# Block-causal attention and gated MLP in one kernel: scores of both heads as single-pass products in the two 64-row halves of the array, seven slots and one output run a pair of heads

## The chip, the cores and the metric

The kernel runs on one core of a Trainium2 chip. The time is device time in microseconds (us) of one execution, from the first instruction to the last, as the runs report it; the number to be predicted is the median over runs of the changed kernel.

The core has five instruction streams that work side by side and meet at semaphores. TensorE (PE in the rows) multiplies: its instructions are a matmul and the load of the weights for it (PEld). VectorE (DVE), ScalarE (ACT) and GpSimd (POOL) work elementwise, and SyncE (SP) only issues DMA transfers here. A tile of numbers lies on 128 partitions; an operand of a matmul is contracted over its partitions, which are the rows of TensorE's array, and the weights' columns are the columns of the array. The results come into eight PSUM banks of 128 x 512 float32.

## The reference

Eight batches, eight heads, 576 tokens, 64 channels a head. The attention is causal in blocks of 64 tokens; its output is the input of a gated MLP that mixes tokens.

```python
B, H, S, D = 8, 8, 576, 64
scores = q @ k.T / sqrt(D)
scores = where(pos_q // 64 >= pos_k // 64, scores, -1e9)
scores = scores - max(scores, axis=-1)
attn = exp(scores)
attn = attn / (sum(attn, axis=-1) + 1e-9)
x = concatenate_heads(attn @ v)                 # [8, 576, 512]

h = maximum(x @ w_in, 0)                        # w_in [512, 1024]
u, v = h[..., :512], h[..., 512:]
v_n = (v - mean(v)) / sqrt(var(v) + 1e-6)       # over the 512 channels
v_s = w_spatial @ v_n + b_spatial               # over the 576 tokens, w_spatial [576, 576]
out = (u * v_s) @ w_out                         # w_out [512, 512]
```

## The kernel before, in words

**Two streams in one program.** The attention goes pair of heads by pair of heads: 8 batches of 4 pairs, written (batch, pair). When a batch has its four pairs, its MLP is cut into 29 groups of products (`moe`: 5 v groups at L468, 8 u groups at L537, 8 spatial groups `ms` at L560, 8 output groups `mo` at L581), and these are put between the attention steps of the next batch's pairs. The MLP of the last batch stands alone at the end.

**Two precisions.** TensorE multiplies whole float32 in several passes and rounded numbers (float32r) in one. Most products are made from two rounded parts of each operand, hi and lo (lo = value - hi), as hi x hi + hi x lo + lo x hi.

**Operands of the scores.** For a pair, q and k of both heads are transposed on the host into one array of 128 rows (64 channels of the one head above 64 channels of the other) by 1216 columns: k in 0 to 576, q in 576 to 1088, and in 1088 to 1216 query block 8 (the last 64 tokens) of both heads, with zeros in the other head's rows. `load_pair` fetches it into `raw`. In batch 0 the scores are made from `raw`, whole, one instruction a tile over the 64 rows of its head (L293). From batch 1 on `prep_pair` makes hi on ScalarE (L222) and lo on VectorE (one of four pieces, two in the first pair) and POOL (L225), and ten DMAs on SyncE (L235 to L243) stack them, for each head, into a tile `st` of 128 rows: k's hi part twice, q's hi above q's lo, and k's lo part twice. Two products over all 128 rows, L296 and L297, then give all combinations of parts for one tile of one head.

**Nine steps a pair.** `TILES` lists the score tiles: (head, query tile), where tile t has 128 queries and needs 128 (t + 1) keys; head 2 stands for query block 8 of both heads. One step is: the scores of a tile into a bank of `ps_s`; a subtraction from the mask and a minimum over the keys on VectorE (L298, or L319 in two halves for block 8), which leaves the masked scores in `p` and the minimum in `nmax`; the exponential with the sum of a row on ScalarE (L325); a small sum and a reciprocal on VectorE (L331, L334); the division on POOL (L338). Three steps later (five in the first 30 steps) `transposes` puts the tile's 128 x 128 blocks through TensorE into a bank of `ps_t`, and a copy takes them to `ptlo` (VectorE, L369), `pthi` or `ptc4` (ScalarE, L376 to L389).

**Two output runs a pair.** `av_lo` (L415) multiplies v by the transposed weights of query tiles 0 and 1, a step after tile (1, 1)'s transposes; `av_hi` (L430, L434, L439) those of the rest, a step after the pair's last transposes. Each uses 64 columns of the array a head; both write the one bank of `ps_av`. `x_evac` copies the bank on ScalarE (L404, rounded) and subtracts on VectorE (L405, the lo part of x).

**What sets the order.** The step loop at the end of the function issues the instructions: scores of step n, work ahead (the next pair's loads and splits, and in batch 0 the decoding of the MLP's weights from float64, `prep_w`, spread over fixed steps), then transposes and output runs that are due, then as many MLP groups as a credit of 29/36 a step allows. From this each engine gets its own row of instructions; a framework then puts in the semaphores, and an instruction that waits holds up all that is behind it on its engine. Buffers are reused in turn: 3 banks for scores, 2 for transposes, 1 for outputs, 2 for the MLP, 4 tiles of `p`, 1 tile each of hi and lo, 3 of `st`. In batch 0, while no MLP runs, its buffers and banks hold more of `p` and `s` in flight (`p_tile`, `s_bank`).

## Time and profile before

| what | value |
|---|---|
| three runs | 762.03, 762.12 and 763.51 us, median 762.12 |
| span of the profiled execution | 760.0 us |
| TensorE busy, share of the span | 750.3 us, 99% |
| VectorE busy | 486.7 us, 64% |
| ScalarE busy | 453.3 us, 60% |
| POOL busy | 316.7 us, 42% |
| chain of waits, share on TensorE | 87% |
| moved by DMA | 96.37 MB in 43814 packets |

The profile is of one execution. Its span, 760.0 us, goes from the first to the last recorded instruction; the runs' own time has 2.1 us more at the median. In rows of the trace "L296" is line 296 of the kernel; `s<-st` is a result and its operands by the program's names (batch, pair and tile numbers left out); `128*64 128x320` is the part of the array in use and the shape of the moving operand. Matmuls are pipelined: a record begins when the instruction starts and its end is modelled, so records overlap, and the cost of a product to TensorE is read from the differences of starts. A product in float32 may leave one record for each pass.

### The profile page before, as it was taken

How to read it: one execution, taken by the hardware profiler on the slowest of the kernel's cores; microseconds unless marked ns; L12 is line 12 of the kernel's file. 1: busy time of each engine (PE TensorE's matmuls, PEld its weight loads, DVE VectorE, ACT ScalarE, POOL GpSimd, SP SyncE). 2: the span in 40 equal slices, each digit the busy share in tenths (PEclk: the TensorE clock that was granted, in tenths of full speed). 3: DMA queues.
4: the chain of work that ended last, by engine and by line, in shares of the span. 5: the costliest groups of instructions: out<-in, count | busy, mean ns of one | idle time of the engine just before them, and what ended most of it. 6: DMA issues, size and time to landing. Idle time of an engine off the chain costs nothing.

```text
span 760.0 us, 16034 instructions
## 1 busy us (share of the span) xinstructions
PE 750.3 (99%) x5284; PEld 648.9 (85%) x5284; DVE 486.7 (64%) x1744; ACT 453.3 (60%) x1236; POOL 316.7 (42%) x478
## 2 busy tenths in 40 slices
PE   8999899999999999999999999999999999999998
PEld 5567798988888889988888889988889988888898
DVE  6997985668545785448755487555865568543641
ACT  6786766655665656566656566655666556654232
POOL 4785775423444325443344334433344423423011
DMA  6477585555465445464355554456454554430001
GB/s 216 138 212 219 146 232 128 129 134 124 114 171 125 115 119 135 133 173 111 85 141 150 141 124 103 127 152 159 106 130 116 139 146 112 92 77 33 0 9 55
DMA packets 43814, 96.37 MB, mean 127 GB/s; under 512 B 6866, under 2 KB 15570, under 8 KB 43732
## 3 DMA queue, kind: packets, MB, share of 16 engines
q1 hardware_dynamic: 43732, 95.35, 48.4%
q8 instruction: 42, 0.69, 0.4%
q14 instruction: 40, 0.33, 0.1%
HBM read 38.18 MB, written 9.44 MB: 63 GB/s over the span
## 4 chain that ended last, share of the span: by engine, by line
PE 87%; DVE 7%; ACT 2%; issue 2%; DMA 1%; SPq 0%; DVEq 0%; ACTq 0%
PE mo L581 14%; PE ms L560 13%; PE mu L537 12%; PE mv L468 11%; PE avh L430 7%; PE t L375 6%; PE s L297 4%; PE s L296 4%; PE s L315 3%; PE avl L415 3%; PE t L382 2%; PE t L368 2%; PE mv L479 1%; PE avh L434 1%; DVE p L298 1%
## 5 line engine op out<-in xcount | busy, mean ns | idle before, releaser
L338 POOL TENSOR_SCALAR p<-p,ssum 128x384 f32<-128x384 f32 (+4 forms) x288 | 175.0, 615 | 252.0 <-DVE ssum L334 96.6
L325 ACT ACTIVATE p<-p,nmax 128x384 f32<-128x384 f32 (+4 forms) x288 | 168.5, 586 | 59.4 <-DVE nmax L298 38.7
L298 DVE CUSTOM_DVE_ANT_0 p<-s,mask 128x128 f32<-128x128 f32 (+3 forms) x256 | 122.7, 486 | 60.2 <-PE s L297 46.4
L537 PE MATMUL mu<-x,wi_hi 128*128 128x288 f32 x512 | 116.3, 303 | 0.5 <-DVE vr L485 0.5
L537 PEld LDWEIGHTS mu<-x,wi_hi 128*128 128x128 f32 x512 | 85.4, 188 | 2.9 <-ACT pthi L376 1.0
L468 PE MATMUL mv<-wi_hi,x 128*128 128x512 f32 x256 | 85.9, 396 | 0.0
L225 POOL TENSOR_TENSOR lo<-raw,hi 128x288 fp32r<-128x288 f32 (+1 forms) x83 | 68.3, 837 | 37.4 <-ACT hi L222 37.4
L331 DVE TENSOR_SCALAR ssum<-ssum 128x1 f32<-128x1 f32 (+1 forms) x224 | 39.1, 175 | 63.8 <-ACT p L325 63.3
L560 PE MATMUL ms<-ws_hi,vh 128*128 128x288 f32 x256 | 78.6, 307 | 0.0
L560 PE MATMUL ms<-ws_hi,vl 128*128 128x288 f32 x256 | 75.4, 294 | 0.0
L560 PE MATMUL ms<-ws_lo,vh 128*128 128x288 f32 x256 | 75.3, 294 | 0.0
L581 PE MATMUL mo<-gh,wo_hi 128*128 128x288 f32 x256 | 74.5, 314 | 0.5 <-ACT gh L568 0.5
L376 ACT COPY pthi<-t 128x384 f32<-128x384 f32 (+1 forms) x128 | 67.8, 530 | 9.9 <-PE t L375 9.1
L568 ACT CAST gh<-u 128x288 fp32r<-128x288 f32 x64 | 27.7, 433 | 75.1 <-DVE u L567 72.7
L297 PE MATMUL s<-st 128*128 128x128 f32 (+1 forms) x224 | 72.3, 323 | 0.0
L296 PE MATMUL s<-st 128*128 128x128 f32 (+1 forms) x224 | 71.5, 321 | 0.0
L375 PE MATMUL t<-ident,p 128*128 128x128 f32 x448 | 70.8, 275 | 0.4 <-POOL p L338 0.3
L537 PE MATMUL mu<-x,wi_lo 128*128 128x288 f32 x256 | 69.7, 295 | 0.0
L581 PE MATMUL mo<-gh,wo_lo 128*128 128x288 f32 x256 | 69.7, 295 | 0.0
L569 POOL TENSOR_TENSOR gl<-u,gh 128x288 fp32r<-128x288 f32 x48 | 38.7, 806 | 64.6 <-ACT gh L568 63.8
L430 PE MATMUL avh<-pthi,v 128*64 128x320 f32 x384 | 61.0, 441 | 0.4 <-DVE x L405 0.4
L375 PEld LDWEIGHTS t<-ident,p 128*128 128x128 f32 x448 | 52.3, 141 | 8.6 <-issue 3.0
(119 smaller groups left out, 1726.0 us busy)
## 6 DMA issues: line engine op xcount, KB each, us to landing
raw<-qk SPq DMA_DIRECT2D x31, 608.0 KB, 5.0
st<-lo SPq DMA_DIRECT2D x112, 144.0 KB, 3.1
st<-hi SPq DMA_DIRECT2D x56, 272.0 KB, 3.2
v<-v SPq DMA_DIRECT2D x32, 320.0 KB, 3.4
outT<-o SPq DMA_DIRECT2D x64, 144.0 KB, 2.5
st<-hi SPq DMA_DIRECT2D x56, 144.0 KB, 3.1
...
```

The costliest lines, as they stand in the source:

```text
L225: (nc.vector if n < (2 if (b, pr) == (1, 0) else 1) else nc.gpsimd).tensor_tensor(out=lo[:, cs], in0=raw[:, cs], in1=hi[:, cs].bitcast(F32 ...
L296: nc.tensor.matmul(ps[:, :n], st[:, qs], st[:, Q8:Q8 + n], start=True, stop=False)
L297: nc.tensor.matmul(ps[:, :n], st[:, qs], st[:, :n], start=False, stop=True)
L298: nc.vector.tensor_tensor_reduce(out=pt[:, :n], in0=ps[:, :n], in1=mask[:, 512 - n:], scale=-0.125, scalar=BIG, op0=ALU.add, op1=ALU.min, ...
L325: nc.scalar.activation(pt[:, :n], pt[:, :n], AF.Exp, bias=mx, scale=-1.0, accum_out=ssum[:, sc:sc + 1])
L338: nc.gpsimd.tensor_scalar(out=pk[:, :nk], in0=pk[:, :nk], scalar1=ssum[:, 2 + sc - k:3 + sc - k], scalar2=1.0, op0=ALU.mult, op1=ALU.mult,)
L375: nc.tensor.transpose(bk[:, c, :], pt[:, c * P:(c + 1) * P], ident)
L430: nc.tensor.matmul(av[js, 0:320], vt[:, c, js], hi[:, j, c, :], start=(c == 0), stop=False)
L468: nc.tensor.matmul(ps, xs[k][:, j, cs], w[:, k, DH:], start=(n == 0), stop=(n == 3 * NC - 1),)
L537: nc.tensor.matmul(ps[:, :HT], w[:, k, ds], xs[k][:, j, zs], start=(n == 0), stop=(n == 3 * NC - 1),)
L560: nc.tensor.matmul(ps[:, :HT], a[:, ds], w[:, k, zs], start=(n == 0), stop=False)
L581: nc.tensor.matmul(ps[:, :HT], w[:, k, es], a[:, k, :], start=(n == 0), stop=(n == 3 * ND - 1),)
```

## The change

**Seven slots in the place of nine steps.** `SLOTS` lists (head, first tile, last tile): slots 0 and 1 hold query tiles 0 and 1 of a head together (in one bank, 128 and 256 columns, and one tile of `p`), slots 2 and 3 tile 2, slots 4 and 5 tile 3, slot 6 query block 8 of both heads. Slot n of a pair makes the minima and exponentials (`exps`) of slot n, the sums and the division (`norm`) of slot n - 1 and the transposes of slot n - 2.

**Scores in runs, half by half.** `scores` has no stacked operands: a head's products take its 64 rows of hi and lo, three products a tile (hi x hi, hi x lo, lo x hi), and the heads take turns, so that a product in rows 0 to 63 stands beside one in rows 64 to 127. Slots 0 to 3 are issued together at slot 0 (18 products), slots 4 and 5 at slot 2 (6 products), query block 8 at slot 5. The tiles `st` and their 280 DMAs go; hi and lo have two tiles each. Batch 0 keeps whole products from `raw`, in the new order.

**One output run a pair**, at slot 2 of the next pair, behind the second run of scores. Its two results lie in the two banks of `ps_t`; `ps_av` goes, scores have four banks. The block-8 part of the weights is multiplied over 128 rows: `c4` is one lasting tile with zeros in its lower 64 rows.

**Order and buffers.** `p` has seven tiles, in batch 0 too. The next pair's split starts at slot 1 and is spread over four slots. The weights' decoding gets new slots: v 3 to 20, u 21 to 32, spatial 31 to 37, output 36 to 42 (before: 5 to 28, 34 to 37, 40 to 51 and 49 to 59, of shorter steps). The credit is 29/28 a slot. Comments go too.

The instructions on TensorE where the output run of pair 0 stands, in the middle of a batch, before (in the names: pair, then tile; the last number is a running one):

```order
L296 MATMUL s_1_3_3889<-st_1_1_3510 128x128
L297 MATMUL s_1_3_3889<-st_1_1_3510 128x128
L382 MATMUL t_1_0_3903<-ident,p_1_0_3745 128x128 x4
L388 MATMUL t_1_0c_3909<-ident,p_1_0_3745 64x128
L430 MATMUL avh_0_3912<-pthi_0_3552,v_0_3124 64x320 x6
L434 MATMUL avh_0_3912<-pthi_0_3552,v_0_3124 64x192 x2
L439 MATMUL avh_0_3912<-ptc_3_0_3553,v_0_3124 64x64 x2
L537 MATMUL mu_0_3_3926<-x_0_2451,wi_hi 128x288
```

And now:

```order
L436 MATMUL mv_3_3691<-wi_hi,x_3_3420 128x512
L265 MATMUL s_1_4_3733<-hi_1_3335 128x512
L265 MATMUL s_1_5_3734<-hi_1_3335 128x512
L265 MATMUL s_1_4_3733<-lo_1_3336,hi_1_3335 128x512
L265 MATMUL s_1_5_3734<-lo_1_3336,hi_1_3335 128x512
L265 MATMUL s_1_4_3733<-hi_1_3335,lo_1_3336 128x512
L265 MATMUL s_1_5_3734<-hi_1_3335,lo_1_3336 128x512
L396 MATMUL avl_0_3741<-ptlo_0_3427,v_0_2999 64x256 x2
L396 MATMUL avl_0_3741<-ptlo_0_3427,v_0_2999 64x128 x2
L405 MATMUL avh_0_3742<-pthi_0_3428,v_0_2999 64x320 x6
L405 MATMUL avh_0_3742<-pthi_0_3428,v_0_2999 64x192 x2
L405 MATMUL avh_0_3742<-c_125,v_0_2999 64x64 x2
```

The scores of tile 3, two heads in turn, stand right ahead of the joined output run, which has four products of `avl` more than the run before had; behind it now come transposes into the same two banks.

VectorE at that place (in another pair), with the semaphores that an instruction waits on, before:

```order
L298 ISA p_2_8_1781,nmax_2_8_1779<-s_2_8_1782,mask 128x512 [waits PE_49,Pool_49]
L298 ISA nmax_2_8_1779 128x1
L331 TENSOR_SCALAR ssum_2_8_1780<-ssum_2_8_1780 128x1 [waits Activation_49]
L334 RECIPROCAL ssum_2_8_1780<-ssum_2_8_1780 128x1 [waits DVE_49]
L405 TENSOR_TENSOR x_2_1800<-avl_2_1795,x_2_1800 128x256 [waits Activation_49]
L319 ISA p_3_0_1821,nmax_3_0_1819<-s_3_0_0_1822,mask 128x288 [waits PE_49,Pool_49]
```

And now:

```order
L296 ISA p_2_4_1662,nmax_2_4_1660<-s_2_4_1540,mask 128x512 [waits PE_49]
L296 ISA nmax_2_4_1660 128x1
L296 ISA p_2_5_1699,nmax_2_5_1697<-s_2_5_1541,mask 128x512 [waits PE_49,Pool_49]
L296 ISA nmax_2_5_1697 128x1
L321 TENSOR_SCALAR ssum_2_4_1661<-ssum_2_4_1661 128x1 [waits Activation_49]
L324 RECIPROCAL ssum_2_4_1661<-ssum_2_4_1661 128x1 [waits DVE_49]
L383 TENSOR_TENSOR x_1_1564<-avl_1_1548,x_1_1564 128x256 [waits Activation_49]
L321 TENSOR_SCALAR ssum_2_5_1698<-ssum_2_5_1698 128x1 [waits Activation_49]
L324 RECIPROCAL ssum_2_5_1698<-ssum_2_5_1698 128x1 [waits DVE_49]
L354 COPY ptlo_2_1570<-t_2_0_1572 128x384 [waits PE_49]
```

The subtraction of `avl` now stands behind the minima of both tiles of 512 columns, and the copy of the next transposes (`ptlo`) behind it.

ScalarE where the next pair's hi is cast, before:

```order
L222 CAST hi_0_1870<-raw_0_1838 128x576
L376 COPY pthi_2_1628<-t_2_6_1840 128x4x128
L325 ACTIVATE p_3_0_1821,ssum_3_0_1820<-p_3_0_1821,nmax_3_0_1819 128x576
L222 CAST hi_0_1870<-raw_0_1838 128x640
L587 COPY o_0_2_1859<-mo_0_2_1846 128x288
```

And now:

```order
L220 CAST hi_0_1791<-raw_0_1757 128x576
L356 COPY pthi_2_1571<-t_2_3_1676 128x3x128
L312 ACTIVATE p_2_6_1729,ssum_2_6_1728<-p_2_6_1729,nmax_2_6_1727 128x576
L220 CAST hi_0_1791<-raw_0_1757 128x640
L555 COPY o_0_0_1694<-mo_0_0_1681 128x288
```

The second cast still stands behind the exponential of query block 8, which now is the last slot of the pair ahead and not its first step.

The diff, cut to its core. Most of the removed lines, which stand in the kernel above, and `exps` and `norm`, which do the same operations as `scores` did before, are left out:

```diff
...
-TILES = [(2, 4), (0, 0), (0, 1), (1, 0), (1, 1), (0, 2), (0, 3), (1, 2), (1, 3)]
-NT = len(TILES)
...
+SLOTS = [(0, 0, 1), (1, 0, 1), (0, 2, 2), (1, 2, 2), (0, 3, 3), (1, 3, 3), (2, 4, 4)]
+NS = len(SLOTS)
+RUN2, LAST = 2, 5
...
-    hl_p = ctx.enter_context(tc.tile_pool(name="hl_p", bufs=1))
-    qk_p = ctx.enter_context(tc.tile_pool(name="qk_p", bufs=3))
+    hl_p = ctx.enter_context(tc.tile_pool(name="hl_p", bufs=2))
...
-    p_p = ctx.enter_context(tc.tile_pool(name="p_p", bufs=4))
+    p_p = ctx.enter_context(tc.tile_pool(name="p_p", bufs=7))
...
-    ps_s = ctx.enter_context(tc.tile_pool(name="ps_s", bufs=3, space=PSUM))
+    ps_s = ctx.enter_context(tc.tile_pool(name="ps_s", bufs=4, space=PSUM))
...
-    ps_av = ctx.enter_context(tc.tile_pool(name="ps_av", bufs=1, space=PSUM))
...
+    c4 = const.tile([P, P], F32, name="c4")
+    nc.gpsimd.memset(c4[64:P, :], 0.0)
...
-            (nc.vector if n < (2 if (b, pr) == (1, 0) else 1) else nc.gpsimd).tensor_tensor(
+            (nc.vector if n == 0 else nc.gpsimd).tensor_tensor(
                 out=lo[:, cs], in0=raw[:, cs], in1=hi[:, cs].bitcast(F32), op=ALU.subtract
             )
             yield
...
+    def operands(b, pr):
+        if b == 0:
+            raw = raws[(b, pr)]
+            return ((raw, raw),)
+        hi, lo = split_of[(b, pr)]
+        return ((hi, hi), (hi, lo), (lo, hi))
+    def s_bank(b, nm, other):
+        if b == 0 and other:
             return ps_m.tile([P, 512], F32, tag="m", name=f"s_{nm}")
         return ps_s.tile([P, 512], F32, tag="s", name=f"s_{nm}")
+    def scores(b, pr, slots):
+        parts = operands(b, pr)
+        for i in slots:
+            banks[(b, pr, i)] = s_bank(b, f"{b}_{pr}_{i}", slots[0] == 4)
+        for i in slots[::2]:
+            o = 0
+            for t in range(SLOTS[i][1], SLOTS[i][2] + 1):
+                n = P * (t + 1)
+                qs = slice(S + t * P, S + (t + 1) * P)
+                for m, (a, k) in enumerate(parts):
+                    for hd in range(2):
+                        js = slice(64 * hd, 64 * hd + 64)
+                        nc.tensor.matmul(
+                            banks[(b, pr, i + hd)][:, o:o + n], a[js, qs], k[js, :n],
+                            start=(m == 0), stop=(m == len(parts) - 1),
+                        )
+                o += n
+    def scores_last(b, pr):
+        parts = operands(b, pr)
+        bk = [s_bank(b, f"{b}_{pr}_{NS - 1}_{z}", False) for z in range(2)]
+        banks[(b, pr, NS - 1)] = bk
+        for z in range(2):
+            for m, (a, k) in enumerate(parts):
+                nc.tensor.matmul(
+                    bk[z][:, :HT], a[:, Q8:], k[:, z * HT:(z + 1) * HT],
+                    start=(m == 0), stop=(m == len(parts) - 1),
+                )
...
+    def av(b, pr):
+        lo, hi = pts.pop((b, pr))
+        vt = vts.pop((b, pr))
+        al = ps_t.tile([P, 512], F32, tag="t", name=f"avl_{b}_{pr}")
+        ah = ps_t.tile([P, 512], F32, tag="t", name=f"avh_{b}_{pr}")
         for c in range(2):
             for j in range(2):
+                js = slice(64 * j, 64 * j + 64)
                 nc.tensor.matmul(
-                    av[64 * j:64 * j + 64, c * P:256], vt[:, c, 64 * j:64 * j + 64],
+                    al[js, c * P:256], vt[:, c, js],
                     lo[:, j, 0:256] if c == 0 else lo[:, j, 256:384],
                     start=(c == 0), stop=(c == 1),
                 )
...
         for c in range(5):
             for j in range(2):
                 js = slice(64 * j, 64 * j + 64)
...
+                q0 = (0, 0, 0, 128, 256)[c]
+                nc.tensor.matmul(
+                    ah[js, q0:320], vt[:, c, js], hi[:, j, c, q0:] if c < 4 else c4[:, js],
+                    start=(c == 0), stop=(c == 4),
+                )
+        x_evac(b, pr, al, 0, 256)
+        x_evac(b, pr, ah, 256, 320)
...
-    spread(chain([prep_w_in(c, 1) for c in range(NC)]), 7 * NC + 1, 5, 28)
-    spread(chain([prep_w_in(c, 0) for c in range(NC)]), 7 * NC + 1, 34, 37)
-    spread(chain([prep_w_sp(c) for c in range(FULL)] + [prep_w_tail()]), 3 * FULL + 5, 40, 51)
-    spread(chain([prep_w_out(c) for c in range(ND)]), 7 * ND + 1, 49, 59)
+    U0 = NPAIR * NS
+    spread(chain([prep_w_in(c, 1) for c in range(NC)]), 7 * NC + 1, 3, U0 - 8)
+    spread(chain([prep_w_in(c, 0) for c in range(NC)]), 7 * NC + 1, U0 - 7, U0 + 4)
+    spread(chain([prep_w_sp(c) for c in range(FULL)] + [prep_w_tail()]), 3 * FULL + 5, U0 + 3, U0 + 9)
+    spread(chain([prep_w_out(c) for c in range(ND)]), 7 * ND + 1, U0 + 8, U0 + 14)
...
+            if i == 1 and b > 0:
+                spread(prep_pair(b, pr), 7, n, n + 4)
         step_background(n)
...
+        if at(n - 1):
+            norm(*at(n - 1))
+        if i == RUN2:
+            if here:
+                scores(*here, (4, 5))
+            if 0 < g <= len(pairs):
+                av(*pairs[g - 1])
+                if g % NPAIR == 0:
+                    gs = moe(pairs[g - 1][0])
+                    queue += gs
+                    rate = len(gs) / (NPAIR * NS)
+        if here and i == LAST:
+            scores_last(*here)
+        if n >= 2 and at(n - 2):
+            transposes(*at(n - 2))
         credit += rate
         while credit >= 1.0 and queue:
             queue.pop(0)()
             credit -= 1.0
+        if at(n):
+            exps(*at(n))
...
```

222 lines of the change are left out of this document (60 added, 162 removed).

## The prediction

> **What bounds the kernel now.** First the busy line of the page and its slices; then busy time over stretches; then the chain of waits; then TensorE's timeline row by row.
>
> ```profile
> PE 750.3 (99%) x5284; PEld 648.9 (85%) x5284; DVE 486.7 (64%) x1744; ACT 453.3 (60%) x1236; POOL 316.7 (42%) x478
> ...
> DVE  6997985668545785448755487555865568543641
> ```
>
> TensorE is busy all through, but matmul records overlap, so this alone would not say that it is the limit. Busy time by stretches (columns: stretch; its length, then PE, PEld, DVE, ACT and POOL busy with instruction counts; clock, DMA share, GB/s):
>
> ```profile
> 40.00:53.00 13.00, 12.63 (x74) 7.15 (x73) 12.76 (x49) 11.38 (x35) 9.48 (x14) 1.00 0.71 184
> 53.00:62.00 9.00, 9.00 (x66) 6.31 (x64) 4.91 (x19) 7.54 (x20) 6.93 (x10) 1.00 0.75 237
> ...
> 85.00:95.00 10.00, 9.14 (x68) 7.46 (x69) 8.74 (x27) 6.72 (x21) 7.45 (x9) 1.00 0.56 162
> ```
>
> ```profile
> 247.84:339.25 91.41, 91.41 (x662) 80.76 (x661) 57.67 (x213) 55.71 (x153) 36.65 (x58) 1.00 0.52 130
> ```
>
> The program has two parts. In the **front**, until about 95 us, VectorE is full or nearly so (12.76 of 13 us before 53, 8.74 of 10 before 95, where TensorE still has gaps of 0.86); TensorE takes what it gets. After it a batch takes 91.41 us, TensorE has no gap, and VectorE is at 63%, ScalarE at 61%, POOL at 40%. There every tenth of a microsecond of TensorE work counts, and work on the others is free as long as it comes in time. In the chain of waits (start, length, what) the first v group of two batches stands at
>
> ```profile
> 156.44 2.74 PE mv L468 x12
> ...
> 702.50 2.96 PE mv L468 x12
> ```
>
> So the stretch from 95 to 702.5 us is the one to cost: 607.5 / 91.41 x 4 = 26.6 pairs of heads, 22.85 us each. What follows 702.5 is the last MLP alone, which the change does not touch.
>
> **The scores.** Before, a tile of one head is two products over all 128 rows (lines 296 and 297). In the timeline (start, length, what), the difference of starts is what a product costs TensorE:
>
> ```profile
> 274.35 0.28 PE L296 MATMUL s<-st 128*128 128x256 f32 x1
> ...
> 274.58 0.34 PE L296 MATMUL s<-st 128*128 128x384 f32 x1
> ...
> 274.93 0.27 PE L366 MATMUL t<-ident,p 128*128 128x128 f32 x1
> ...
> 277.12 0.40 PE L296 MATMUL s<-st 128*128 128x512 f32 x1
> ...
> 277.58 0.29 PE L537 MATMUL mu<-x,wi_hi 128*128 128x288 f32 x1
> ```
>
> ```profile
> 286.01 0.31 PE L296 MATMUL s<-st 128*128 128x128 f32 x1
> 286.15 0.28 PE L297 MATMUL s<-st 128*128 128x128 f32 x1
> 286.26 0.52 PE L375 MATMUL t<-ident,p 128*128 128x128 f32 x3
> ```
>
> Two products of 256 columns take 274.58 - 274.35 = 0.23 us, of 384 columns 0.35, of 512 columns 0.46; of 128 columns one takes 0.11 (286.15 to 286.26). One of each width: 0.115 + 0.175 + 0.23 + 0.11 = 0.63 us. Before: two products x two heads = 4 x 0.63 = 2.52 us a pair. After: three products (hi x hi, hi x lo, lo x hi) x two heads = 6 products over 64 rows each. If the two halves of the array run side by side, a pair costs 3 x 0.63 = 1.89 us, **0.63 less**. If they take turns it costs 6 x 0.63 = 3.78, 1.26 more. The rows decide how far I believe in side by side. Batch 0 already multiplies with 64 rows (L293: whole float32, two passes an instruction, so two records):
>
> ```profile
> 12.89 1.22 PE L293 MATMUL s<-raw 64*128 64x128 f32 x8
> 14.04 0.33 PE L375 MATMUL t<-ident,p 128*128 128x128 f32 x1
> ```
>
> ```profile
> 26.24 0.49 PE L293 MATMUL s<-raw 64*128 64x128 f32 x2
> 26.66 0.55 PE L375 MATMUL t<-ident,p 128*128 128x128 f32 x3
> 27.14 0.70 PE L293 MATMUL s<-raw 64*128 64x256 f32 x2
> 27.76 0.66 PE L375 MATMUL t<-ident,p 128*128 128x128 f32 x4
> ```
>
> Alone, 128 columns take 0.42 us and 256 columns 0.62, so two heads one after the other would take 2.08. At 12.89 both widths of both heads took 1.15: the halves do run side by side. A gap stays: a float32 pass streams a column in 0.83 ns (next fence), a single-pass product in 0.23 / 512 = 0.45 ns. Two halves at single pass are shown by no row here. I take side by side, since a pair of halves reads no more rows a column than one product over 128 rows at the same speed does.
>
> A second question is whether the next weights of the same half are loaded behind its running product:
>
> ```profile
> 16.44 1.77 PE L293 MATMUL s<-raw 64*128 64x384 f32 x4
> 18.14 0.44 PE L375 MATMUL t<-ident,p 128*128 128x128 f32 x2
> ```
>
> Here one head has two passes of 384 and two of 512 columns. At 0.83 ns they stream 0.32 + 0.32 + 0.43 + 0.43 = 1.50 us, and from 16.44 to 18.14 is 1.70: one load of 0.11 (a 128-column product is load-bound at 0.11) and 0.09 for leaving the mode. Three more loads in the open would make 2.03. So loads hide.
>
> The Trainium skill (TensorE: Matmul & The Clock Gate, Part 3, "What overlaps and what doesn't") says that a weight load overlaps running matmuls only where the row group differs; by it the three later loads would lie open, which 1.70 us does not bear out. The sum with it is rival B.
>
> **Changes of the array's form.** These are what the change pays. Output runs use 64 columns:
>
> ```profile
> 270.11 0.27 PE L388 MATMUL t_0c<-ident,p 128*64 128x128 f32 x1
> 270.31 1.84 PE L430 MATMUL avh<-pthi,v 128*64 128x320 f32 x12
> 271.97 0.49 PE L434 MATMUL avh<-pthi,v 128*64 128x192 f32 x4
> 272.40 0.33 PE L439 MATMUL avh<-ptc,v 64*64 64x64 f32 x4
> 272.66 0.40 PE L537 MATMUL mu<-x,wi_hi 128*128 128x288 f32 x1
> 272.90 0.29 PE L537 MATMUL mu<-x,wi_lo 128*128 128x288 f32 x1
> 273.03 0.29 PE L537 MATMUL mu<-x,wi_hi 128*128 128x288 f32 x1
> ```
>
> In: 270.11 to 270.31 is 0.20 where a transpose takes 0.11, +0.09; six pass pairs of 320 columns are 6 x 0.267 = 1.60 and took 1.66, +0.06 for the first load. Inside, into 64 rows: 0.43 for 0.32, +0.11, and the load of 0.05. Out: +0.09, and the first product waits 0.24 instead of 0.13 for its weights, +0.11. Before, a pair has two runs: 2 x 0.15 in, 2 x 0.20 out, 0.16 inside: 0.86 us. After: a run of 18 score products (in 0.09 + 0.11 = 0.20; out to transposes 0.09 + 0.06 = 0.15), a second of 6 (in 0.20), the joined output run behind it (in 0.15, nothing inside, out to transposes 0.15): 0.85. Once a batch a first score product stands alone in an output group, one more in and out, 0.40 / 4 = 0.10 a pair (20 changes a batch become 22). Together +0.10. The other products of the seven slots (query block 8, transposes, output) are the same in number and width.
>
> TensorE: -0.63 + 0.10 = **-0.53 us a pair, x 26.6 = -14.1 us**. The pair (1, 0) and part of (1, 1) lie in the front and bring nothing.
>
> **The copies.** The 280 copies into `st` (ten a pair) go. Their one trace on a path is in the front:
>
> ```profile
> 82.90 2.36 DMA st<-lo
> ```
>
> It is 2.36 us of the chain; VectorE behind it is nearly full anyway, so 0 to 2.4, I take -1.0. Elsewhere the copies wait for nobody on TensorE, nothing to gain. SyncE keeps `v` ahead of `raw`, and `v` now waits for the joined output run in slot 2.
>
> **Waits that replace them.** Two chains get short. The output run takes both transpose banks, so the next transposes wait for the subtraction that empties the first; on VectorE it stands behind both 512-column minima. And ScalarE's second cast of the next pair's operands stands behind the exponential of slot 6, VectorE's `lo` behind that, and the next 18-product run needs `lo`. Groups by form (after the bar: busy us, mean ns):
>
> ```profile
> L298 DVE CUSTOM_DVE_ANT_0 p<-s,mask 128x512 f32<-128x512 f32 x64 | 44.0, 688 | 17.9 <-PE s L297 15.3 <-POOL p L338 0.9
> ...
> L225 DVE TENSOR_TENSOR lo<-raw,hi 128x512 fp32r<-128x512 f32 x28 | 27.1, 967 | 5.0 <-DMA st<-hi 3.9 <-ACT o L587 0.4
> ...
> L319 DVE CUSTOM_DVE_ANT_0 p<-s,mask,nmax 128x288 f32<-128x288 f32 x32 | 16.4, 513 | 3.4 <-PE t L375 0.5 <-DVE nmax L319 0.2
> ...
> L405 DVE TENSOR_TENSOR x<-avl,x 128x256 fp32r<-128x256 f32 x32 | 13.2, 411 | 1.2 <-ACT x L404 1.2
> ```
>
> ```profile
> L325 ACT ACTIVATE p<-p,nmax 128x576 f32<-128x576 f32 x32 | 24.9, 777 | 11.7 <-DVE nmax L319 10.7 <-DVE ssum L334 0.7
> L222 ACT CAST hi<-raw 128x640 fp32r<-128x640 f32 x28 | 20.1, 716 | 0.0
> ```
>
> First chain: 0.69 + 0.69 + 0.41 and the two small sums between, about 2.1 us, under an output run of 2.7 (0.64 + 1.60 + 0.32 + 0.11): 0.6 to spare. Second: 0.51 + 0.78 + 0.72 + 0.97 = 3.0 us and four hand-overs, under two transposes (0.33, 0.44) and two groups of twelve products at 0.13 (1.6 each), 4.0 us: under 1 us to spare. The lag from scores to transposes, two slots now, is no shorter: slot 0 has two transposes, two groups, the second run and the output run ahead, 0.8 + 3.2 + 0.9 + 2.8 = 7.7 us, and before three of nine steps, 22.85 / 3 = 7.6 us. Without cover, each would cost what it is late, up to one VectorE instruction of 0.97 us in a pair. Bounds 0 to 0.97 x 26.6 = 26; I take 0.1 a pair, **+2.5**, near the lower end because both sums end under their cover.
>
> **The front.** VectorE does the same operations; the weights of u are decoded over more slots, fewer minima are in flight (seven buffers of `p`), and the first v group now comes behind pair (0, 3)'s output. VectorE idles 4.1 us from 53 to 62: that much could be won, and as much lost if the smaller pool starves it. -4 to +5; I take 0.
>
> **Sum**, against the profiled execution's span of 760.0: -14.1 - 1.0 + 2.5 = -12.6, 747.4 us. The median of the runs, 762.1, lies 2.1 above the span: **749.5 us**.
>
> **The rivals.**
> *A, slower: the halves take turns* at single pass. The float32 rows leave room, as each pass uses half the rate. Price 1.26 + 0.10 = 1.36 a pair, x 26.6 = +36, with the other terms 800 us. It decides from where two halves together take 1.25 times what one takes alone; at 1.3 the scores are 2.46 a pair, -0.06 + 0.10, and the time is 764. The Trainium skill (TensorE: Matmul & The Clock Gate, Part 3, "Measured speedup vs the span model") has four row tiles at 3.07 times one, an estimate of 1.3 for two halves if each tile gives 0.77; no run here shows it yet.
>
> *B, slower: loads of a half lie open.* Widths above 128 get 0.11 a product, 128 gets 0.05: 3 x 0.38 = 1.14 a pair, so +0.51 + 0.10, x 26.6 = +16: 780 us. The row at 16.44 speaks against it.
>
> *C, the waits eat the gain*: 0.5 us a pair on either chain is 13.3 instead of 2.5: 760.3, and with 0.7 it is slower, 766. For it: slacks under 1 us, and the v groups' VectorE work in bursts. Against: VectorE at 63%, and no TensorE gap now.
>
> *D, the change doesn't do what it says*: only if TensorE's queue pulled the heads apart; the order shows them in turn, save the one product a batch counted above. And the front could lose 5 us: 754.5.
>
> **How the numbers follow.** Forecast 0.70, its own range 743 to 756; A (in part or whole) 0.10; B 0.04; C 0.12; a front far worse 0.04. Range: at the low end the front wins 4 and no wait is left (743), and a few more if the pair (1, 0) and the lost copies count fully, 739; at the high end 763, which takes in C to its middle and leaves most of A and B out. A measurement tells 0.2%, 1.5 us, from no change. Faster: 0.70 + half of C + the smaller front losses = 0.77; same 0.05; slower 0.18.
>
> **What would show it.** Score records of 64 rows that start in pairs within 0.02 us: three pairs of 512 columns in 0.7 us are the forecast, in 1.4 A, in 1.0 B. A batch of 89 to 90 us between first v groups bears out the sum; 91.4 or more, with gaps of TensorE ahead of transposes (released by VectorE's x) or of score products (by VectorE's lo), is C. The first v group of the second MLP between 150 and 159 us shows the front as taken. A time above 763 would make the prediction wrong, and so would one below 739, which only a front that I misread could give.

## The result: slower by 0.6%

The median rose from 762.20 to 766.26 us (nine runs each, 764.45 to 769.88 with the change); the ratio is 1.0063, with a 95% interval of 1.0045 to 1.0081. The forecast was 749.5, faster. The profiled execution has a span of 763.8 us against 760.0.

From the page of the changed kernel, the busy line and VectorE's slices:

```profile
PE 740.3 (97%) x5508; PEld 636.0 (83%) x5508; DVE 471.9 (62%) x1743; ACT 436.1 (57%) x1236; POOL 318.4 (42%) x480
...
DVE  6985984548745577547764577455874557742641
```

TensorE is busy 10 us less and the span is 3.8 us longer. The chain of waits shows where the two parts of the program now meet (start, length, what; the first v group of the second MLP and of the last):

```profile
165.63 2.75 PE mv L436 x12
...
706.32 2.94 PE mv L436 x12
```

Before, these stood at 156.44 and 702.50. So the second MLP begins 9.2 us later, and 5.4 of that are won back by the last one: the **front lost about 9, the steady part gained about 5**. (The border between the two is here the start of the second MLP.) Busy time over stretches (columns as in the prediction: stretch; length, PE, PEld, DVE, ACT, POOL; clock, DMA share, GB/s), the changed kernel:

```profile
8.87:11.19 2.32, 0.27 (x2) 0.03 (x1) 1.92 (x11) 1.63 (x6) 2.22 (x6) 1.00 1.02 383
37.60:39.00 1.40, 0.36 (x4) 0.15 (x3) 1.40 (x7) 0.58 (x2) 1.40 (x3) 1.00 0.93 318
41.40:44.70 3.30, 3.30 (x13) 2.05 (x14) 2.60 (x15) 2.60 (x10) 1.96 (x3) 0.51 0.64 200
57.51:60.58 3.07, 0.00 (x0) 0.00 (x1) 2.91 (x9) 1.57 (x7) 3.07 (x5) 1.00 0.00 0
61.80:66.00 4.20, 4.20 (x23) 2.34 (x24) 2.10 (x9) 2.78 (x9) 1.08 (x3) 0.61 0.25 98
85.00:110.00 25.00, 18.86 (x138) 15.85 (x138) 24.61 (x76) 15.54 (x43) 12.24 (x14) 1.00 0.26 81
0.00:130.00 130.00, 115.03 (x731) 83.92 (x732) 100.15 (x361) 88.24 (x240) 82.70 (x112) 0.97 0.39 124
256.26:346.89 90.63, 89.81 (x693) 78.67 (x693) 56.24 (x213) 52.80 (x152) 37.13 (x59) 1.00 0.19 56
```

and the kernel before:

```profile
0.00:130.00 130.00, 123.92 (x782) 92.67 (x782) 108.26 (x379) 94.17 (x257) 87.11 (x114) 1.00 0.64 183
85.00:110.00 25.00, 24.14 (x184) 20.71 (x184) 22.22 (x68) 17.31 (x49) 18.42 (x20) 1.00 0.76 206
```

Until 130 us TensorE is idle 130 - 115.03 = 15.0 us instead of 6.1; of the 8.9 more, 5.3 lie between 85 and 110, where VectorE is full (24.61 of 25). What TensorE waited for most in these 130 us was the division on POOL that comes ahead of a tile's transposes (waited for: us in all, times, longest). The changed kernel:

```profile
PE t L352 <- POOL p L326: 7.2, 5, 3.1
```

and the kernel before:

```profile
PE t L382 <- POOL p L338: 2.0, 2, 1.6
...
PE t L375 <- POOL p L338: 0.3, 2, 0.2
```

And something that the profile of before does not show at all: after two of the idle stretches (37.60 and 57.51) the granted clock fell to half for some 3 to 4 us. Over the nine runs the mean clock is 0.988 to 0.998 (the kernel before: 1.000 in its profile, 0.999 or 1.000 in the 17 runs beside e1), and the time goes with it: a line through them has 0.53 us for each 0.001 and meets clock 1.000 at 763.0.

Where the front loses shows in the start of the last product of each pair's output run (us, from the traces; e13 is an experiment below):

| pair | (0, 0) | (0, 1) | (0, 2) | (0, 3) | (1, 0) | (1, 3) |
|---|---|---|---|---|---|---|
| before | 23.3 | 36.8 | 51.9 | 62.1 | 88.3 | 155.8 |
| change | 22.4 | 35.9 | 50.2 | 66.7 | 97.4 | 164.9 |
| e13 | 30.6 | 45.4 | 63.0 | 77.7 | 104.9 | 175.4 |

Through the first three pairs the change is ahead. It loses 6.3 us up to the output of (0, 3), with the wait of 3.1 us for POOL and the second stretch of half clock, and 4.5 more up to that of (1, 0); after that the distance stays at 9 to 11. Until the output of (1, 0) VectorE has done about the same work in both (77.2 and 76.2 us), but has stood idle 20.2 us instead of 12.1.

The steady batch is 256.26 to 346.89, 90.63 us, instead of 91.41. The score products, TensorE's timeline (start, length, what; x2 is one product in each half):

```profile
269.81 0.33 PE L265 MATMUL s<-hi 64*128 64x128 f32 x2
269.98 0.28 PE L265 MATMUL s<-lo,hi 64*128 64x128 f32 x2
...
270.96 0.33 PE L265 MATMUL s<-hi,lo 64*128 64x384 f32 x2
271.22 0.66 PE L352 MATMUL t<-ident,p 128*128 128x128 f32 x4
```

```profile
277.20 0.39 PE L436 MATMUL mv<-wi_hi,x 128*128 128x512 f32 x1
277.52 0.50 PE L265 MATMUL s<-hi 64*128 64x512 f32 x2
277.86 0.40 PE L265 MATMUL s<-lo,hi 64*128 64x512 f32 x2
278.09 0.40 PE L265 MATMUL s<-hi,lo 64*128 64x512 f32 x2
278.42 0.65 PE L396 MATMUL avl<-ptlo,v 128*64 128x256 f32 x4
```

The halves do run side by side: a pair of 512-column products takes 278.09 - 277.86 = 0.23, no more than one. What was a wait in that batch (waited for: us in all, times, longest; ends of matmuls are modelled, and by the starts it is 0.81 and 0.24, together **1.05**):

```profile
PE t_6c L366 <- ACT pthi L356: 0.7, 1, 0.7
PE t L352 <- DVE x L383: 0.2, 1, 0.2
```

For one batch, the differences of starts of all matmuls, added up by what the earlier one is (us; a column adds up to the batch's period, waits included; the last two columns are experiments below):

| | before | change | scores stacked (e10) | joined output run alone (e14) |
|---|---|---|---|---|
| MLP | 55.1 | 56.4 | 55.6 | 55.0 |
| scores | 13.5 | 12.7 | 14.0 | 13.8 |
| transposes | 10.2 | 9.9 | 9.0 | 8.9 |
| output | 12.6 | 11.7 | 11.4 | 11.4 |

### The profile page after: what moved, and what is told of

Read it like the earlier page. It is cut to its first block, busy times and chain, and to the rows that moved or that the text cites. A ratio compares the mean times of both kernels' runs of the same rounds, so it can differ in the third digit from the quotient of the medians.

```text
span 763.8 us, 15854 instructions
## 1 busy us (share of the span) xinstructions
PE 740.3 (97%) x5508; PEld 636.0 (83%) x5508; DVE 471.9 (62%) x1743; ACT 436.1 (57%) x1236; POOL 318.4 (42%) x480
## 4 chain that ended last, share of the span: by engine, by line
PE 81%; DVE 8%; ACT 5%; POOL 2%; issue 2%; DMA 1%; SPq 0%; ACTq 0%; DVEq 0%; POOLq 0%
PE mo L549 14%; PE ms L528 13%; PE mu L505 10%; PE t L352 10%; PE mv L436 10%; PE s L265 7%; PE avh L405 6%; PE s L277 3%; PE avl L396 2%; ACT p L312 2%; PE mv L447 1%; DVE st L457 1%; POOL p L326 1%; PE ms L533 1%; PE ms L532 1%
## 5 line engine op out<-in xcount | busy, mean ns | idle before, releaser
L326 POOL TENSOR_SCALAR p<-p,ssum 128x128 f32<-128x128 f32 (+4 forms) x288 | 177.9, 630 | 209.9 <-DVE ssum L324 173.9
L312 ACT ACTIVATE p<-p,nmax 128x128 f32<-128x128 f32 (+4 forms) x288 | 166.9, 581 | 59.6 <-DVE nmax L296 47.3
L296 DVE CUSTOM_DVE_ANT_0 p<-s,mask 128x128 f32<-128x128 f32 (+3 forms) x256 | 115.4, 484 | 62.8 <-PE s L265 62.7
L352 PE MATMUL t<-ident,p 128*128 128x128 f32 x768 | 124.6, 278 | 10.5 <-POOL p L326 7.2
L352 PEld LDWEIGHTS t<-ident,p 128*128 128x128 f32 x768 | 90.6, 141 | 27.8 <-POOL p L326 12.3
L356 ACT COPY pthi<-t 128x512 f32<-128x512 f32 (+1 forms) x128 | 67.0, 525 | 29.1 <-PE t L352 28.8
L535 DVE TENSOR_TENSOR u<-ms,u 128x288 f32<-128x288 f32 x64 | 29.3, 458 | 78.1 <-PE ms L533 78.0
L321 DVE TENSOR_SCALAR ssum<-ssum 128x1 f32<-128x1 f32 (+1 forms) x224 | 37.2, 166 | 50.8 <-ACT p L312 50.8
L405 PE MATMUL avh<-pthi,v 128*64 128x320 f32 (+1 forms) x512 | 67.9, 407 | 0.0
L405 PEld LDWEIGHTS avh<-pthi,v 128*64 128x64 f32 x512 | 36.0, 138 | 24.2 <-issue 0.3
```

Source lines behind the costliest of these rows:

```text
L296: nc.vector.tensor_tensor_reduce(out=pt[:, o:o + n], in0=bk[:, o:o + n], in1=mask[:, 512 - n:], scale=-0.125, scalar=BIG, op0=ALU.add, op1 ...
L312: nc.scalar.activation(pt[:, o:o + n], pt[:, o:o + n], AF.Exp, bias=mx, scale=-1.0, accum_out=ssum[:, r:r + 1],)
L326: nc.gpsimd.tensor_scalar(out=pt[:, o:o + n], in0=pt[:, o:o + n], scalar1=ssum[:, 2 + r:3 + r], scalar2=1.0, op0=ALU.mult, op1=ALU.mult,)
L352: nc.tensor.transpose(bk[:, c * P:(c + 1) * P], pt[:, c * P:(c + 1) * P], ident)
L356: nc.scalar.copy(hi[:, hd, 0:n, (t - 2) * P:(t - 1) * P], bk[:, :n * P].rearrange("p (c q) -> p c q", q=P),)
L405: nc.tensor.matmul(ah[js, q0:320], vt[:, c, js], hi[:, j, c, q0:] if c < 4 else c4[:, js], start=(c == 0), stop=(c == 4),)
```

## Experiments

The edits are shown against the changed kernel, those of e13, e14, e17 and e18 against the kernel before. The kernel before ran beside all of them; ratios are to it.

### The two halves: e1, e5

```diff
-                for m, (a, k) in enumerate(parts):
-                    for hd in range(2):
+                for hd in range(2):
+                    for m, (a, k) in enumerate(parts):
```

> The change, but the products of a tile come head after head (three of the one half, then three of the other) instead of in turn. Theory S (the halves run side by side and the loads of a half are hidden): a pair costs 6 x 0.63 = 3.78 us of score products instead of 1.89, so +1.89 in each of the 28 pairs after batch 0: about +53, span near 817; products of 512 columns of one half start 0.23 apart. Rival A (the halves already share the array in part, as rival A of the prediction at a factor of 1.3): the pair costs 2.46 now, so only +1.3 a pair, span near 800. Rival B (loads of a half lie open): starts of one half 0.34 apart at 512 columns, and more than +60.

One run: 772.22 us, and the period is 352.77 - 261.93 = 90.84, only 0.2 longer. I had not expected that. Its chain and timeline:

```profile
261.93 2.75 PE mv L436 x12
...
352.77 2.75 PE mv L436 x12
```

```profile
275.49 0.33 PE L265 MATMUL s<-hi 64*128 64x128 f32 x2
275.65 0.28 PE L265 MATMUL s<-lo,hi 64*128 64x128 f32 x2
```

Although three products of one half stand ahead of the other's in program order, the records still come in pairs, 0.01 apart (under 0.005 in the change): TensorE starts the other half's product while the first half's wait. So this edit didn't take side by side away; e5 does, by reading both heads from one half:

```diff
-                        js = slice(64 * hd, 64 * hd + 64)
+                        js = slice(64 * hd, 64 * hd + 64) if b == 0 else slice(0, 64)
```

> The change, but from batch 1 on both heads' score products read the lower 64 rows (so the second head's scores are those of the first: the time alone counts). After the kernel with head after head kept the two halves side by side by itself (period of a batch 90.83 instead of 90.63), this takes the second half away. Theory S (two halves at the price of one is what the 64-row products gain, and the next load of the same half is hidden): +1.89 us in each pair, the period of a batch 98.2 and the span about 816; products of 512 columns start 0.23 apart. Rival A (halves shared the array only in part): a smaller rise, at a factor of 1.3 +1.3 a pair and a period near 96. Rival B (loads of a half lie open): starts 0.34 apart at 512 columns and a period above 100.

One run: 808.87 us.

```profile
268.91 2.75 PE mv L436 x12
...
366.05 2.75 PE mv L436 x12
```

```profile
290.58 0.73 PE L265 MATMUL s<-hi 64*128 64x512 f32 x2
291.15 0.63 PE L265 MATMUL s<-lo,hi 64*128 64x512 f32 x2
291.62 0.62 PE L265 MATMUL s<-hi,lo 64*128 64x512 f32 x2
```

The period is 97.14. No wait is left in it, so TensorE's work grew by 97.14 - (90.63 - 1.05) = 7.56, 1.89 us a pair: exactly 3 x 0.63. (The 1.05 is the change's waits.) Two products of one half take 291.62 - 291.15 = 0.47, that is 0.23 each, without an open load. Theory S holds; rivals A and B of the prediction fall. So does the rule on loads (the Trainium skill, TensorE: Matmul & The Clock Gate, Part 3, "What overlaps and what doesn't") for this case: the same row group's next load was hidden here.

### What the 64-row products are worth: e10

The ten stacking copies a pair and the two 128-row products come back, in the same slots and runs (`p` has four tiles and `st` two, for space):

```diff
+                if b > 0:
+                    for hd in range(2):
+                        st = stacked[(b, pr, hd)]
+                        for m in range(2):
+                            nc.tensor.matmul(
+                                banks[(b, pr, i + hd)][:, o:o + n], st[:, qs],
+                                st[:, Q8:Q8 + n] if m == 0 else st[:, :n],
+                                start=(m == 0), stop=(m == 1),
+                            )
```

> The change with the scores from batch 1 on made as before it: two products over all 128 rows from stacked operands, fetched by ten DMAs a pair, in the same runs and slots (for space p has four tiles, not seven, and the stacked operands two). By the starts in the two traces, the 64-row products save 0.63 us a pair and pay 0.56 of it back (0.09 at each of two entries, 0.21 inside and behind the first run, 0.11 inside the second, 0.06 at the first transpose): the stacked kernel's TensorE work should be 0.1 to 0.3 us a batch longer than the change's, the period 90.6 to 91.2. If the 64-row products are worth what the prediction had (0.63 less, entries already counted before as much): a period of 92 to 93.

One run: 768.22 us, but a shorter period:

```profile
261.41:351.40 89.99, 89.84 (x662) 81.16 (x661) 56.91 (x213) 53.72 (x152) 36.51 (x58) 1.00 0.52 132
```

TensorE's work is 0.4 a batch more than the change's 90.63 - 1.05 = 89.58, near what was expected; but no wait is left, so the batch ends 0.64 sooner. In the table the 64-row products save 1.3 in the scores and give 0.8 back in the MLP, whose last product ahead of each of nine runs takes 0.09 more. That leaves 0.1 us a pair. (The waits may also depend on the number of `p` tiles; that was not tried apart.)

### The waits: e2

```diff
-            bk = bank(f"{i}c4")
-            nc.tensor.transpose(bk[0:64, 0:P], pt[:, 4 * P:S], ident)
-            nc.scalar.copy(c4[0:64, :], bk[0:64, 0:P])
+            last_p[(b, pr)] = pt
...
             if 0 < g <= len(pairs):
+                transpose_tail(*pairs[g - 1])
                 av(*pairs[g - 1])
```

> The change, but the lone 64-column transpose of query block 8 (t_6c) stands right ahead of the next output run instead of behind the four other transposes of that block. Theory W (once a batch this transpose waits 0.8 us for a bank that ScalarE empties behind exponentials; with a second, smaller wait behind the output run this is the 1.0 us a batch that the steady part lost to waits): the period from batch to batch falls from 90.63 to about 89.7, the time by 6 us, to about 760. Rival (the wait is slack that the next instruction takes up; TensorE is held by something else): the period stays within 0.2 of 90.6 and the time within 2 us of the change's.

768.13 us, ratio 1.0071 (1.0053 to 1.0089). From the chain:

```profile
259.44 2.77 PE mv L442 x12
...
349.74 2.78 PE mv L442 x12
```

The period is 90.30. The wait of t_6c is gone, but only 0.33 of 0.8 came back: between single-pass products this transpose costs 0.12 more in each of four pairs. The theory named the wait rightly and its worth wrongly. The time even rose; these runs had more half clock (mean clock 0.985), all of it in the front in the one with a profile, but for the end of the span.

### The joined output run alone: e14, e17

The change's output run on the kernel before, from batch 1 on, with the rest over 128 rows:

```diff
-            if ti == TILES.index((1, 1)):
+            if ti == TILES.index((1, 1)) and tg < NPAIR:
                 due.append((n + (2 if n < 45 else 1), av_lo, tg))
...
+        if b > 0:
+            al = ps_t.tile([P, 512], F32, tag="t", name=f"avl_{b}_{pr}")
...
-                        av[js, 256:320], vt[0:64, c, js], c4[:, js], start=False, stop=True
+                        av[js, 256:320], vt[:, c, js], c4[:, js], start=False, stop=True
```

From step 45 on the runs that are due come ahead of the step's transposes, and `c4` is one tile with zeros below.

> The kernel before, with another part of the change alone: from batch 1 on the two output runs of a pair are one, and its rest is multiplied over 128 rows from one lasting tile with zeros. Theory J (this part is the whole of the change's steady gain): by the rows of the prediction 0.15 + 0.20 less for one run fewer and 0.16 less inside, 0.5 us a pair or 2.0 a batch, a period near 89.5 instead of 91.41, and with the front untouched 749 to 754 us. Rival (the joined run waits for its second bank and for the copies, or the steady gain of the change came from the scores): period 90.8 or more, 758 or more.

754.37 us, ratio 0.9888 (0.9863 to 0.9912): **faster than both kernels**.

```profile
251.21:340.35 89.14, 89.14 (x661) 81.33 (x661) 59.43 (x214) 55.66 (x153) 36.94 (x58) 1.00 0.53 133
```

2.27 us a batch, 0.57 a pair, against 0.51 from the prediction's rows. So a batch of the change is made up of: joined run -2.27 (91.41 to 89.14), seven slots with stacked scores +0.85 (89.14 to 89.99), 64-row scores with their waits +0.64 (89.99 to 90.63); together -0.78. The 0.85 holds all else in which e10 and e14 differ, buffers and banks too; 0.6 of it is in the MLP's products and 0.2 in the scores of the table.

Its front was not as before (TensorE busy 118.33 of the first 130), so e17 joins from batch 2 on only.

> The kernel before with the joined output run from batch 2 on; batches 0 and 1 keep their two runs a pair (the rest over 128 rows is used throughout). If the joined run in batch 1 costs the front its 5 us (the low part of the output comes later, while VectorE is full): TensorE's idle time until 130 us is back at 6 to 7 us, the period stays 89.15, and 24 pairs at 0.57 us less give 13 us less than before: 748 to 751. If the front of the joined kernel lost for another reason (the lasting tile of zeros, the order of the output run against the transposes): 753 to 756.

757.57, ratio 0.9934 (0.9921 to 0.9948): slower than e14, above both expected ranges, and TensorE busy 118.83 of 130. So it is not the joined run in batch 1 that costs the front some 5 us. What is left of the edit there is the lasting tile, with the rest over 128 rows; why that, or the order that follows from it, costs so much is open.

### The front, one repair at a time: e3, e4, e6, e7, e9

e3: the low part of pair (0, 3)'s output is made in its own pair, and two v groups come ahead.

```diff
+        if (g, i) == (NPAIR - 1, 4):
+            av_lo(*pairs[g])
+        if n == U0:
+            queue += moe(0)
+        if n in (U0, U0 + 1):
+            queue.pop(0)()
...
```

> The change, but in batch 0 the low part of the output of its last pair is made in a run of its own before that pair is through (as before the change), and the first two v groups are issued two slots earlier, so that the MLP of batch 0 starts near 53 us instead of 67. Theory F1 (the joined output run delays the first v group, VectorE idles from 53 to 80 us and is full from 80 to 110, and TensorE then waits for it): 3 to 8 us less, time 758 to 763, with TensorE idle of 85 to 110 us down from 6.1 to under 3. Rival F2 (the front loses by the pieces of lo on POOL, by fewer tiles of p and scores in flight, and by the decoding of the weights; the start of the MLP does not matter): within 1.5 us of the change.

769.09, ratio 1.0083 (1.0069 to 1.0098). The first v group came at 61 us instead of 67; 53 was expected. TensorE's idle time from 85 to 110 fell from 6.1 to 3.6 us, but it now stood still 6.1 us at 72, behind VectorE's normalisation of v. The gain that F1 promised did not come: an earlier first v group alone, as far as this edit moved it, brings nothing.

e4: three of four pieces of `lo` on VectorE for (1, 0) and (1, 1).

```diff
-            (nc.vector if n == 0 else nc.gpsimd).tensor_tensor(
+            (nc.vector if n < (3 if (b, pr) in ((1, 0), (1, 1)) else 1) else nc.gpsimd).tensor_tensor(
```

> The change, but for the pairs (1,0) and (1,1) three of the four pieces of lo are made by VectorE and one by POOL (in the change one and three). Theory F2 (TensorE's longest idle time, 3.1 us before the transposes at 60.6 us, is a division on POOL that stands behind three pieces of lo, 2.4 us): the wait falls to about 1.5 us and the time by 1 to 2 us. Theory F1 (the idle VectorE until 80 us and its full stretch after it set the front): the time stays within 1 us, since the end of the front is set later by VectorE, to which this adds 3.2 us.

764.64, ratio 1.0031 (1.0009 to 1.0053). TensorE is busy 119.38 of the first 130 us, 4.4 more than in the change, some of it at half clock. F2's size is about right, though the interval overlaps the change's.

e6: the second pair's operands are fetched ahead of `v`.

```diff
     load_pair(0, 0)
+    load_pair(0, 1)
     load_v(0, 0)
...
```

> The change, but the operands of the second pair are fetched ahead of the two loads of v. Theory C (TensorE waits 2.0 to 2.3 us for this load at 9 us, and such an idle stretch is often followed by 4 to 10 us at half the granted clock, as at 12 to 21 us in three of the kernels tried): the idle stretch is gone, the clock stays at 1.00 until 35 us, and the median of the time falls by 2 to 4 us, to 762 to 764. Rival (VectorE sets the front and takes up what TensorE gains there): TensorE's gap goes, but the time stays within 1 us.

766.69, ratio 1.0051 (1.0035 to 1.0066). The idle stretch at 9 us is gone and the clock is 1.00 until 58, but the time stays, as the rival had it; its reason, VectorE, is not shown by this.

e7: VectorE relieved in batch 0's MLP.

```diff
-                nc.vector.tensor_copy(vh, vr)
-                nc.vector.tensor_tensor(
+                (nc.scalar.copy if b == 0 else nc.vector.tensor_copy)(vh, vr)
+                (nc.gpsimd if b == 0 else nc.vector).tensor_tensor(
```

(and `ptlo` of the pairs (1, 0) and (1, 1) copied by ScalarE)

> The change, but in batch 0's MLP the normalised v is cast by ScalarE and its lo part made by POOL, and ScalarE copies ptlo for the pairs (1,0) and (1,1): about 7.6 us of work taken off VectorE between 67 and 110 us. Theory V (VectorE, full from 80 to 110 us, is what TensorE waits for there, 6.1 us idle from 85 to 110): that idle time falls to under 3 us and the time by 3 to 5 us, to 761 to 763. Rival (the order of the front and POOL's divisions set it): within 1.5 us, as POOL gets 3.4 us more.

767.13, ratio 1.0071 (1.0045 to 1.0098). VectorE is no longer full from 85 to 110 (22.47 of 25), and TensorE is still idle 6.6 us there, but for another reason. In the change it waited there for POOL's division (3.9 us) and VectorE's minima (2.2); in e7 it is one wait for a copy on ScalarE:

```profile
PE t_6c L366 <- ACT pthi L356: 6.2, 1, 6.2
```

That copy stands behind two casts that the edit put on ScalarE, a copy between them that waits 1.4 us for POOL's new work, and two exponentials that wait 1.5 us for VectorE's minima. So the edit moved the wait, and theory V stays undecided. ScalarE has waits of its own already in the change, for loads of the spatial weights (in brackets idle before, and what ended it):

```profile
70.03 0.67 ACT L114 CAST ws_hi<-rws 128x576 fp32r<-128x576 f32 x1 [1.53 <-DMA rws<-w_spT]
72.44 0.67 ACT L114 CAST ws_hi<-rws 128x576 fp32r<-128x576 f32 x1 [1.24 <-DMA rws<-w_spT]
76.14 0.67 ACT L182 CAST ws_a<-rwt 128x576 fp32r<-128x576 f32 x1 [1.74 <-DMA rwt<-w_spT]
```

e9 fetches each block of the spatial weights one block ahead.

```diff
+        load(0)
+        yield
+        load(1)
+        yield
+        for c in range(FULL):
+            yield from split(ws_hi[:, c, :], ws_lo[:, c, :], rs[c])
+            if c + 2 <= FULL:
+                load(c + 2)
+                yield
...
```

> The change, but each block of the spatial weights is fetched one block ahead of its use. Theory F3 (the decoding of the spatial and output weights, pressed into fewer slots, makes ScalarE's in-order queue wait 4.5 us for these loads between 68 and 76 us, and behind it stand the relu and the square roots of the v groups, then VectorE, then TensorE's transposes and scores of 85 to 110 us): ScalarE's waits for the loads go, TensorE's idle time from 53 to 130 us falls from 9.9 to about 6, and the median by 2 to 4 us, to 762 to 764. Rival V (VectorE has too much work there anyway): ScalarE's waits go, TensorE's idle time stays within 1.5 us and the time within 1 us.

767.39, ratio 1.0072 (1.0055 to 1.0088). ScalarE's waits for these loads fell from 4.5 to 1.5 us; the time did not, and TensorE's idle time from 53 to 130 us rose from 9.7 to 11.1. F3 falls.

### Several at once: e8, e11, e12

e8 has the edits of e2, e4, e6 and e7; e11 those of e2, e4, e6 and e9; e12 adds this to e11:

```diff
-    spread(chain([prep_w_out(c) for c in range(ND)]), 7 * ND + 1, U0 + 8, U0 + 14)
+    spread(chain([prep_w_out(c) for c in range(ND)]), 7 * ND + 1, U0 + 9, U0 + 17)
```

> The change with the second pair's operands fetched first, three pieces of lo on VectorE for the pairs (1,0) and (1,1), VectorE relieved in batch 0's MLP, and the lone transpose ahead of the output run. If the loss of the change is in the front (idle TensorE of 15 us until 130 us against 6 before, and the half clock that follows the long gaps): idle time until 130 us under 9, the clock above 0.997, and with a period of 90.3 a time of 755 to 759, faster than the kernel before by 0.4 to 0.9%. If the front's loss is in the order of the seven slots itself: 762 or more.

> The change with the second pair's operands fetched first, three pieces of lo on VectorE for the pairs (1,0) and (1,1), the lone transpose ahead of the output run, and the spatial weights fetched one block ahead. If the front's loss comes from engines that wait for loads and pieces in order: TensorE idle until 130 us under 9 us, clock above 0.997, time 757 to 760, 0.3 to 0.7% under the kernel before. If it lies in the order of the slots (first v group at 67 instead of 53 us): 762 or more.

> The same as the one before it, and the decoding of the output weights starts one slot later and is spread over eight slots instead of six (its VectorE work of 10 us then lies from about 92 to 118 us, as before the change, instead of 91 to 108). If VectorE's full stretch up to 110 us is what holds TensorE: 1 to 3 us less than the one before it; if the loads were the whole cause: within 1 us of it.

763.27 (1.0007, 0.9995 to 1.0019), 765.17 (1.0023, 1.0008 to 1.0037) and 763.86 (1.0018, 1.0006 to 1.0030). All are better than the change and none better than before; TensorE stays idle 14.7 to 16.5 us until 130 in their profiles. What is gained is about the 2 us of e2's period and some of e4. The one run of e11 that kept clock 1.000 took 761.53.

### What the change dropped: e13, e18, e15, e16

The kernel before has an arrangement for batch 0 that the change takes out in the main: five steps from scores to transposes, and the idle MLP's buffers and banks for `p` and scores (eight buffers beside its four tiles of `p`; of the banks, the change still borrows those for tile 3's scores). e13 takes all of it out of the kernel before:

```diff
-T_BOOT, T_LAG, BOOT_STEPS = 5, 3, 30
+T_BOOT, T_LAG, BOOT_STEPS = 3, 3, 30
...
-    p_p = ctx.enter_context(tc.tile_pool(name="p_p", bufs=4))
+    p_p = ctx.enter_context(tc.tile_pool(name="p_p", bufs=5))
...
-        if b == 0 and n <= DH:
+        if False:
...
-        if len(banks) <= 35 and (len(banks) - 1) % 5 >= 3:
+        if False:
...
```

> The kernel before, with one part of the change alone: batch 0 has no longer lag (three steps, not five), and its p and score tiles use their own buffers (five of p) and banks, not the MLP's. Theory B (the front of the change loses because this arrangement, which covers the way from scores over minimum, exponential, sum and division to the transposes while no MLP is there to fill TensorE, was dropped): the kernel before loses 5 to 10 us, to 767 to 772, TensorE's idle time until 130 us rises from 6 to 12 or more, and the granted clock falls below 1.00 there. Rival O (the front loses by the seven slots and the late first v group): within 2 us of 762.

779.45, ratio 1.0207 (1.0163 to 1.0252), 17 us over its neighbours. A part of that is the clock: of its four runs the one at clock 1.000 took 773.79, still 11 us more than before. In its profile TensorE is idle 12.2 of the first 130 us, and the clock is below 1 as in the change:

```profile
0.00:130.00 130.00, 117.80 (x640) 78.99 (x641) 98.59 (x335) 81.59 (x221) 71.44 (x98) 0.93 0.55 162
```

e18 takes the lag alone (its first line, and the low output run one step after its transposes throughout).

> The kernel before with three steps from scores to transposes in batch 0 instead of five; the MLP's buffers and banks are still used for p and scores. If the lag is the half that matters of what the change dropped: 768 to 778, near the 779 of the kernel without both. If the buffers are: within 2 us of 762.

764.08, ratio 1.0016 (1.0006 to 1.0027), clock 1.00:

```profile
0.00:130.00 130.00, 123.55 (x755) 90.06 (x756) 102.00 (x370) 92.36 (x249) 83.61 (x112) 1.00 0.62 179
```

So in the kernel before the buffers and banks carry the front, or they and the lag together; the lag alone is worth 1.1 us (764.08 - 763.03). That it is the change's loss too, the table of output runs bears out only in part. e13 is 7.3 us late at its first pair, most of it half clock (8 to 21 us in its profile), loses 3.8 more up to (0, 2) and 4.5 from there to (0, 3). The change, which drops most of the same, loses nothing up to (0, 2), and 6.3 from there to (0, 3). e15 gives the change a lag of three slots in its first three pairs (and their output run comes a slot later), e16 has that and the edits of e4 and e6.

```diff
-        if n >= 2 and at(n - 2):
-            transposes(*at(n - 2))
+        while done <= n - (3 if n < 3 * NS + 2 else 2) and at(done):
+            transposes(*at(done))
+            done += 1
...
```

> The change, with three slots instead of two from scores to transposes in the first three pairs (and their output run a slot later). Theory B: TensorE's idle time until 53 us falls from 5.3 us to 3.5 or less, the clock stays at 1.00 there, and the time falls by 2 to 4 us. Rival O: within 1 us, since the time is set later, between 53 and 110 us.

> The change with the longer lag in the first three pairs, the second pair's operands fetched first, and three pieces of lo on VectorE for the pairs (1,0) and (1,1). If these three are the front's loss: TensorE idle until 130 us under 9 us, time 757 to 760. If the front is set by the order of the slots after 53 us: 762 or more.

764.99 (1.0026, 1.0009 to 1.0042) and 764.30 (1.0025, 1.0009 to 1.0041). The lag wins some 1.3 us of the median, but the signs of theory B did not come: TensorE is busy 115.49 of 130, its idle time until 53 us rose from 5.3 to 8.1, and the clock there was 0.94. e16 is no better. More buffers and banks for batch 0 of the change were not tried.

Over all eleven kernels with repairs, the first v product of the second MLP starts between 163.8 and 170.4 us in the profile; in the change it starts at 165.4 and before at 156.3. No repair won back more than 1.7 of the 9 us.

## Why the prediction was wrong, step by step

Its sum was -14.1 for TensorE, -1.0 for the copies, +2.5 for waits and 0 for the front, -12.6 in all. Measured: +3.8 in the profile. Of these 16.4 us the front has 10.2 (9.2 lost, where the copies' 1.0 was to be won) and the steady part 6.2 (5.4 gained instead of 11.6).

- **The scores** (-0.63 a pair) were right: side by side, loads hidden (e5: 1.89 a pair, to the hundredth). The changes of form were nearly so: by e10 the 64-row runs give back 0.5 of the 0.63, and the joined run is worth 0.57 where the rows gave 0.51. But I never set them against each other part by part. The prediction's own 0.20 + 0.15 + 0.20 + 0.10 for the score runs is 0.65, as much as the scores save; all but 0.1 a pair of the gain was the joined run's. e10 and e14 show it.
- **TensorE's term** came out at (91.41 - 90.63 + 1.05) / 4 = 0.46 a pair instead of 0.53. Missing from the sum was what the rest of the change costs, its seven slots above all: 0.85 a batch, 0.21 a pair, between e14 and e10.
- **Waits** were 1.05 a batch, 0.26 a pair, instead of 0.1: 6.9 us instead of 2.5, inside the bounds of 0 to 26. Neither chain that I named was the main one. The first (the subtraction of avl) waited 0.24 once a batch, the second never. The larger wait (0.8) is that of the lone transpose of block 8 for a bank that ScalarE's `pthi` copy empties, behind three exponentials:

```profile
274.54 0.30 PE L366 MATMUL t_6c<-ident,p 128*64 128x128 f32 x1 [0.65 <-ACT pthi L356]
```

- **The front** is the step that failed. Taken as 0, with bounds of -4 to +5 from VectorE's idle 4.1 us, and -1.0 for the copies, it lost 9.2. I costed VectorE's work, which hardly changes, and not when that work can be done: by the output of (1, 0) VectorE had stood idle 8 us more than before. I gave the chain through POOL no price: TensorE's transposes waited 7.2 us for its division instead of 2.3, the longest time (3.1) behind three pieces of lo for the next pair. With two of these pieces moved to VectorE (e4) the output of (0, 3) came 2.5 us earlier, that of (1, 3) only 1.4: later waits took up the rest. The prediction named "fewer minima are in flight" in passing and gave it no price; that is worth 17 us in the kernel before, 11 in the one run at full clock (e13, with the lag). It may be part of the change's loss between (0, 2) and (0, 3), where e13 loses too, but through (0, 2) the change has none of it, and after (0, 3) it loses 4.5 where e13 loses 1.0. What holds the change there is not shown.
- **The clock** was 1.00 in every stretch of before, and I took it as given. In the profiles half clock follows stretches in which TensorE is idle, and by the line through the nine runs that is about 0.53 x 7 = 3.7 us of the median's 4.1, an estimate. (In the ten repaired kernels with six runs or more the slope is 0.25 to 0.62.)
- Rivals A and B had no part in it. C was right in kind (a wait took a share of the gain), D in kind for the front, at 5 where 9 came.

Open: which single part of the change makes its front lose. Of eleven kernels with repairs the best was 3.0 us below the change, most of that won in the steady part, and e14 and e17 show that a small edit elsewhere adds 5 us to TensorE's idle time in the front.
